# Half of layer 1 of four more blocks as seven multiplications, in the two PSUM banks of the plain groups

## The chip, the cores and the metric

The kernel runs on one core of a Trainium2 chip: TensorE (PE, matrix products, results only to PSUM), VectorE (DVE), ScalarE (ACT), GpSimd (POOL) and SyncE (SP, which here issues most DMAs). The metric is the device time of one execution in microseconds. A kernel's time is the median of its runs.

## The reference

Sliding-window causal attention (window 64, 8 batches, 8 heads, 576 tokens, head size 64), then a feed-forward layer with squared ReLU on the 4608 x 512 result.

```python
scores = (q @ k.T) / sqrt(64)                 # per batch and head
mask   = (rel >= 0) & (rel < 64)              # rel = row - column
attn   = softmax(where(mask, scores, -1e9))
x      = (attn @ v) as (4608, 512)            # tokens x (heads * 64)
h      = maximum(x @ w_in, 0.0)               # w_in:  512 x 2048
out    = (h * h) @ w_out                      # w_out: 2048 x 512
```

## The kernel before

**Blocks.** The tokens are handled in nine blocks of 512: block g below 8 is the first 512 tokens of batch g, block 8 gathers the last 64 tokens of every batch. Matmuls are in fp16 with fp32 sums. Inputs come in by DMA as fp32 into "st" tiles (ten buffers), POOL casts them to fp16 (L120), q and k are transposed by DMA (L242, issued by SP) into tiles of the pool tpool (tag "T", five buffers). The odd 64-token offsets of v need a second, shifted copy: six casts of 64 partitions on POOL for one block (shift_v_parts, L233).

**The main loop.** After a prologue for blocks 0 to 2, the loop over n = 1 to 8 does layer 2 of block n, layer 1 of block n+1 and attention of block n+2 in one step. The order on every engine is the order in which the code emits instructions. A string per step says which group is emitted at which slot: "1" a group of layer 1, "2" a group of layer 2. The dictionary "at", filled by put(i, work), holds what is emitted ahead of slot i: scores with their exp (Sc, L288 and L295), masking (M, L302), weighted sums and normalisation (A: L318, L325, L328), transposes of the result into xT (X, L344 and L118), and the sums that layers 1 and 2 need. Input parts are loaded a few at a time, by a running total over all slots (next_part).

**Layer 1, plain (F1).** A group f is 128 of the 2048 hidden features for 512 tokens: four matmuls of 512 columns into one of two PSUM banks (ps_f1, tag "f1"; L358), a ReLU on DVE into an "hr" tile (three buffers, L361), the square on ACT into h2 (L362). 16 groups make a block.

**Layer 1 in seven products (L1S).** In step 7 (layer 1 of block 8) x and w_in are cut into 2 x 2 pieces, and seven products of sums of pieces take the place of eight (the Winograd form). m is one of four sets of two groups of the first feature half and two of the second. Each product of a set (product1, L480) is four matmuls of 256 columns. The sums of pieces of w_in are W_sum, those of x are X_sum, both on DVE (L422). Products are added in PSUM in the order 5, 1, 6, 2, 7, 3, 4 over three banks a, b, c, with copies between banks by ACT (L118): product 5 is kept in SBUF (kept5), product 1 is copied from a to b, b to c after product 6, and c to a after product 7. done5 adds the kept product on DVE (L515). A list "later" puts off ReLUs and squares, and catch_up emits some after each group. In step 7 two sets go together, in the banks of attention and ps_f1.

**Layer 2 in seven products (L2S).** From step 2 on, layer 2 works likewise: for each of two token halves s, seven products of eight 256-column matmuls (L446), in the order 1, 2, 6, 5, 7, 3, 4, into the banks "chain" and "side". Its sums of h are S_sum (DVE, L422), 1024 columns each, four for each s; sums of w_out (T_sum) are made once in step 1. Scaled results go by ACT (L562) and DVE (L565) to the output tile.

**Where sums lie.** T sums fill the tile wsum, S sums of both halves fill hsum, W sums take four T tiles. S1 to S3 of s = 0 are made at the end of the step before.

## Time and profile before

| | |
|---|---|
| median of 3 runs | 296.46 us (296.03 to 297.95) |
| profiled execution | 298.29 us, its span 296.6 us |
| granted TensorE clock | 1.000 |
| busy: PE, DVE, ACT, POOL | 287.0, 225.5, 178.1, 126.7 us |
| layer 1, plain: L358 | 496 matmuls of 128x512, 122.7 us busy |
| layer 1, seven products: L480 | 112 matmuls of 128x256 |
| ReLU L361, square L362 | 0.686 and 0.630 us each |
| S sums L422 | 0.72 to 0.77 us each |

The span is the time from the first to the last instruction; the rest of an execution lies around it. Step 2 starts near 107 us, step 3 at 137, step 4 at 166, step 5 at 196, step 6 at 226, step 7 at 255 and step 8 at 280. Matmuls are pipelined, so a line of the timeline shows each longer than its share of PE; how long a run of them takes is read from one start to the next, or from the chain of work that ended last.

### The profile page before, as it was taken

The page shows a single profiled execution, that of the slowest core. Times are in us where ns is not written, and L with a number is a line of the kernel's source. Part 1 is how long each engine was busy: PE and PEld are TensorE (multiplying, and loading weights), DVE is VectorE, ACT ScalarE, POOL GpSimd, SP SyncE. Part 2 cuts the span into 40 slices and gives each one's busy share as a digit, 9 for nine tenths or more (in the row PEclk, how much of TensorE's full clock was granted, in tenths as well). Part 3 has the DMA queues.
Part 4 walks back from the last instruction along what each step waited for, and adds up shares of the span by engine and source line. Part 5 has one row for each costly group of instructions (what it writes and reads, how often), then busy time and mean ns, then how long its engine had stood idle before and what let it go on. Part 6 is the DMA issues. An engine that isn't in the chain of part 4 may idle for free.

```text
span 296.6 us, 7511 instructions
## 1 busy us (share of the span) xinstructions
PE 287.0 (97%) x2953; PEld 185.0 (62%) x2953; DVE 225.5 (76%) x395; ACT 178.1 (60%) x308; POOL 126.7 (43%) x215
## 2 busy tenths in 40 slices
PE   7889999999999999999999999999999999999994
PEld 5443445555545456666666666666666666888883
DVE  3667637679877788888778878887798889878781
ACT  3556667598465756575656465646564655687821
POOL 4567868973494358228416722923223000000002
PEclk9999999999999999999999999999999999999999
DMA  7899999999999997999899999899998014201015
GB/s 203 227 314 389 404 356 253 314 252 169 185 259 171 201 206 114 213 185 242 161 210 214 209 158 237 171 198 193 201 220 222 4 27 100 87 5 73 0 73 142
DMA packets 143651, 56.07 MB, mean 189 GB/s; under 512 B 127712, under 2 KB 136160, under 8 KB 143616
## 3 DMA queue, kind: packets, MB, share of 16 engines
q1 hardware_dynamic: 143232, 55.00, 86.0%
q0 software_dynamic: 144, 0.39, 0.6%
q8 instruction: 23, 0.38, 0.6%
q10 hardware_dynamic: 240, 0.20, 0.3%
q14 instruction: 12, 0.10, 0.1%
HBM read 38.80 MB, written 9.44 MB: 163 GB/s over the span
## 4 chain that ended last, share of the span: by engine, by line
PE 88%; SPq 6%; DMA 4%; POOL 1%; ACT 0%; issue 0%; DVE 0%
PE hps L358 34%; PE chain L446 14%; PE side L446 12%; PE ops L394 5%; PE at L480 4%; PE at L318 4%; DMA wsum<-in_moe_w_in_dram 4%; PE at L288 3%; PE side L394 2%; PE chain L394 2%; SPq L180 2%; PE more L446 2%; SPq L173 2%; PE at L344 2%; PE at L446 1%; PE tr L257 1%
## 5 line engine op out<-in xcount | busy, mean ns | idle before, releaser
L362 ACT ACTIVATE h<-hr 128x512 f16<-128x512 f32 x128 | 80.1, 630 | 80.0 <-DVE hr L361 79.6
L358 PE MATMUL hps<-xT,w_in_sb 128*128 128x512 f16 x496 | 122.7, 379 | 0.6 <-POOL w_in_sb L120 0.4
L361 DVE TENSOR_SCALAR hr<-hps 128x512 f32<-128x512 f32 x127 | 85.8, 686 | 31.3 <-PE hps L358 28.2
L358 PEld LDWEIGHTS <-w_in_sb 128*128 128x128 f16 x500 | 46.7, 98 | 43.2 <-issue 1.4
L446 PEld LDWEIGHTS <-hsum 128*128 128x128 f16 x448 | 43.0, 98 | 11.8
L120 POOL CAST v_ev<-st_v 128x512 f16<-128x512 f32 x31 | 22.3, 720 | 43.6 <-DMA st_v<-in_v_dram 43.6
L446 PEld LDWEIGHTS <-h 128*128 128x128 f16 x336 | 32.7, 98 | 8.3 <-issue 0.4
L120 POOL CAST k<-st_k 128x512 f16<-128x512 f32 x33 | 21.2, 644 | 36.6 <-DMA st_k<-in_k_dram 34.0
L295 ACT ACTIVATE pm<-at 128x1024 f16<-128x1024 f32 x35 | 34.1, 1015 | 2.2 <-PE at L288 2.2
L387 POOL DMA_DIRECT2D out_dram<-osb x3 | 1.8, 596 | 63.2 <-ACT osb L562 61.8
L328 DVE TENSOR_TENSOR xs<-at,rden 128x512 f16<-128x512 f32 x36 | 24.9, 691 | 1.2
L302 DVE TENSOR_TENSOR pm<-pm,mask 128x1024 f16<-128x1024 f16 x32 | 24.1, 765 | 2.0 <-ACT pm L295 1.9
L422 DVE TENSOR_TENSOR hsum<-h 128x1024 f16<-128x1024 f16 x28 | 21.6, 770 | 5.2 <-ACT h L362 5.1
L446 PE MATMUL chain<-wsum,hsum 128*128 128x256 f16 x192 | 24.9, 273 | 0.0
L233 POOL CAST v_od<-st_v 64x512 f16<-64x512 f32 x30 | 22.6, 755 | 1.6
L120 POOL CAST q<-st_q 128x512 f16<-128x512 f32 x28 | 19.2, 709 | 6.1 <-DMA qT<-q 3.5
L394 PEld LDWEIGHTS <-h 128*128 128x128 f16 x128 | 11.6, 98 | 12.2
L318 PEld LDWEIGHTS <-pm 128*64 128x64 f16 x576 | 11.2, 110 | 6.9 <-DVE pm L302 3.0
L118 ACT ACTIVATE xT<-at 128x512 f16<-128x512 f16 x22 | 12.8, 587 | 4.0 <-PE at L344 4.0
L394 PE MATMUL ops<-w_out_sb,h 128*128 128x512 f16 x64 | 14.8, 380 | 0.0
L318 PE MATMUL at<-v_ev,pm 128*64 128x65 f16 x384 | 13.7, 198 | 0.2 <-ACT v_ev L118 0.2
L562 ACT ACTIVATE osb<-chain 128x256 f32<-128x256 f32 x36 | 13.4, 372 | 0.3 <-PE chain L446 0.3
(118 smaller groups left out, 386.2 us busy)
## 6 DMA issues: line engine op xcount, KB each, us to landing
st_k<-in_k_dram SPq DMA_DIRECT2D x37, 256.0 KB, 3.9
out_dram<-osb SPq DMA_DIRECT2D x32, 256.0 KB, 3.1
st_q<-in_q_dram SPq DMA_DIRECT2D x29, 256.0 KB, 4.7
st_v<-in_v_dram SPq DMA_DIRECT2D x28, 256.0 KB, 4.1
w_st<-in_moe_w_in_dram SPq DMA_DIRECT2D x4, 512.0 KB, 6.2
wsum<-in_moe_w_in_dram SPq DMA_DIRECT2D x4, 512.0 KB, 10.2
hsum<-in_moe_w_out_dram SPq DMA_DIRECT2D x4, 512.0 KB, 7.9
wsum<-in_moe_w_out_dram SPq DMA_DIRECT2D x4, 512.0 KB, 9.2
```

Of the source, the lines that this page charges most:

```text
L120: engine.tensor_copy(out=out, in_=in_)
L233: nc.gpsimd.tensor_copy(out=od[g][to:to + 64, m, :, 0:D], in_=st["v", g, c][of:of + 64, :].rearrange("p (h d) -> p h d", h=H))
L295: nc.scalar.activation(out=p[:, hh, :] if apart else p[:], in_=sc[hh] if apart else both[:], func=AF.Exp, scale=1.0 / float(D) ** 0.5)
L302: nc.vector.tensor_tensor(out=p[:], in0=p[:], in1=m.unsqueeze(1).broadcast_to([P, 2, 512]), op=ALU.min)
L318: nc.tensor.matmul(a[jj * 64:(jj + 1) * 64, hh, jp * VW:jp * VW + D + 1], pm[g, hp][:, hh, j * 64:(j + 1) * 64], vsel, start=True, stop=True)
L328: nc.vector.tensor_tensor(out=x[:].rearrange("p j h d -> p h j d"), in0=a[:, :, :, 0:D], in1=rden[:].unsqueeze(3).broadcast_to([P, 2, 4, D ...
L358: nc.tensor.matmul(hps[:], w_in_sb[:, c, f * P:(f + 1) * P], xT[g][:, c, :], start=(c == 0), stop=(c == DMC - 1))
L361: nc.vector.tensor_scalar(out=hr[:], in0=hps[:], scalar1=0.0, scalar2=None, op0=ALU.max)
L362: nc.scalar.activation(out=h2[g][:, f, :], in_=hr[:], func=AF.Square)
L394: nc.tensor.matmul(f2[g, ts][:], h2[g][:, f, ts * P:(ts + 1) * P], w_out_sb[:, f, :], start=(f == 0), stop=(f == FFC - 1))
L422: (engine or nc.vector).tensor_tensor(out=out, in0=a, in1=b, op=op)
L446: nc.tensor.matmul(to, a[:, f, :], b[:, f, :], start=start and f == 0, stop=f == HF - 1, skip_group_check=True)
```

## The change

In steps 3 to 6 (layer 1 of blocks 4 to 7, the fifth to the eighth) the groups with f % 8 below 4 are made as two sets of seven products (pair_step), the other eight groups stay plain. In the order strings "7" is a product step. A set uses the two banks of ps_f1, with c in the place of a: product 7 is read by done5 before product 4 is added, and no copy from c to a is left. Product 5 is kept in columns 256 to 511 of w_out_sb, which only T_sum and the plain layer 2 of step 1 read; the results go to "hr" tiles. All ReLUs of done5 outputs are on ACT, at once after their group (two deferred ACT operations may follow each group).

S sums lie in half of hsum and are used for both s in turn, so those for s = 0 are now made at the start of their own step, those for s = 1 after the products of s = 0. The last block's s = 1 has the other half of hsum, in which W sums of the first two sets lie before. W sums of the other two sets lie in two T tiles. X sums lie in the "qk" tiles.

In the steps with product steps attention starts at slots 2 and 20 of 36, with longer distances to masking, weighted sums and transposes. The shifts of v come behind the third q cast of the next block.

```diff
-    S_sb = hsum[:].bitcast(FP16).rearrange("p a b -> p (a b)").rearrange("p (k c d) -> p k c d", k=4, c=8)
+    S_sb = hsum[:, 0:4, :].bitcast(FP16).rearrange("p a b -> p (a b)").rearrange("p (k c d) -> p k c d", k=4, c=8)
+    S2_sb = hsum[:, 4:8, :].bitcast(FP16).rearrange("p a b -> p (a b)").rearrange("p (k c d) -> p k c d", k=4, c=8)
...
-    def s_of(k, s):
-        return S_sb[:, k - 1, :, 128 * s:128 * s + 128]
+    def s_of(k, two=False):
+        return S2_sb[:, k - 1] if two else S_sb[:, k - 1]
...
@@ -432,14 +433,15 @@
             minus(t_of(4), b_of(1, 0), t_of(2))
 
     def S_sum(g, k, s):
+        w = g == B and s == 1
         if k == 1:
...
+    def W_sum(k, pair):
+        if (pair, k) not in wsums:
+            if pair == 0:
+                t = hsum[:, 3 + k, :].bitcast(FP16)
+                wsums[pair, k] = t.rearrange("p (c f) -> p c f", c=2)
+            else:
+                t = tpool.tile([P, HP, 512], FP16, name="wS", tag="T")
+                for i in range(2):
+                    wsums[pair, k + i] = t[:, 2 * i:2 * i + 2, :]
+        cols = slice(pair * 512, pair * 512 + 512)
+        w = wsums[pair, k]
+        a, b, op = {1: (w_of(1, 0)[:, :, cols], w_of(1, 1)[:, :, cols], ALU.add),
+                    2: (wsums.get((pair, 1)), w_of(0, 0)[:, :, cols], ALU.subtract),
+                    3: (w_of(0, 0)[:, :, cols], w_of(1, 0)[:, :, cols], ALU.subtract),
+                    4: (w_of(0, 1)[:, :, cols], wsums.get((pair, 2)), ALU.subtract)}[k]
+        minus(w, a, b, op)
 
     def X_sum(g, k):
...
         if k not in xsums:
-            t = apool.tile([P, 2, 512], FP16, name="xS", tag="pm", bufs=4)
-            xsums[k] = t[:, 0, :].rearrange("p (c t) -> p c t", c=2)
+            t = apool.tile([P, 2, 512], FP16, name="xS", tag="qk")
+            for i in range(2):
+                xsums[k + i] = t[:, i, :].rearrange("p (c t) -> p c t", c=2)
         a, b = {1: (x_of(g, 0, 1), x_of(g, 0, 0)), 2: (x_of(g, 1, 1), xsums.get(1)),
                 3: (x_of(g, 1, 1), x_of(g, 0, 1)), 4: (x_of(g, 1, 0), xsums.get(2))}[k]
         minus(xsums[k], a, b)
...
+                w = wsums[m // 2, a][:, cc, f % 512:f % 512 + P] if isinstance(a, int) else a[:, cc, f:f + P]
+                nc.tensor.matmul(to[:, u * HX:(u + 1) * HX], w, b[:, cc, :],
...
-    kept5 = {}
...
-        def piece32(name):
-            return stp.tile([P, 512], FP32, name=name, tag="st")
+        def piece32():
+            return opool.tile([P, 512], FP32, name="hr", tag="hr")
+
+        def five(m):
+            t = w_out_sb[:, 4 * (m % 2):4 * (m % 2) + 4, HC:2 * HC].bitcast(FP32)
+            return t
...
         def done(m, i, j, bank):
-            hr = piece32("ls")
+            hr = piece32()
...
         def done5(m, i, j, bank, relu_on_act):
-            y = piece32("ls")
-            nc.vector.scalar_tensor_tensor(out=y[:], in0=bank, scalar=1.0, in1=kept5[m][:],
+            y = piece32()
+            nc.vector.scalar_tensor_tensor(out=y[:].rearrange("p (a b) -> p a b", a=4),
+                                           in0=bank.rearrange("p (a b) -> p a b", a=4), scalar=1.0, in1=five(m),
                                            op0=ALU.mult, op1=ALU.add)
             if relu_on_act:
                 later["act"].append(lambda: nc.scalar.activation(out=y[:], in_=y[:], func=AF.Relu))
...
-        to, lhs, rhs, start = {5: (1, wsums.get(1), xsums.get(1), True), 1: (0, w_of(0, 0), x_of(g, 0, 0), True),
-                               2: (0, w_of(0, 1), x_of(g, 1, 0), False), 6: (1, wsums.get(2), xsums.get(2), False),
-                               7: (2, wsums.get(3), xsums.get(3), False), 3: (1, wsums.get(4), x_of(g, 1, 1), False),
-                               4: (0, w_of(1, 1), xsums.get(4), False)}[p]
+        to, lhs, rhs, start = {5: (1, 1, xsums.get(1), True), 1: (0, w_of(0, 0), x_of(g, 0, 0), True),
+                               2: (0, w_of(0, 1), x_of(g, 1, 0), False), 6: (1, 2, xsums.get(2), False),
+                               7: (2, 3, xsums.get(3), False), 3: (1, 4, x_of(g, 1, 1), False),
+                               4: (2, w_of(1, 1), xsums.get(4), False)}[p]
         for m in two:
             product1(banks[m % 2][to], m, lhs, rhs, start)
         for m in two:
             a, b, c = banks[m % 2]
             if p == 5:
-                kept5[m] = piece32("p5")
-                copy(nc.scalar, kept5[m][:], b)
+                copy(nc.scalar, five(m), b.rearrange("p (a b) -> p a b", a=4))
...
             elif p == 6:
                 copy(nc.scalar, c, b)
             elif p == 7:
-                copy(nc.scalar, a, c)
-                later["dve"].append(lambda m=m, c=c: done5(m, 1, 1, c, m < 2 or RELU[0]))
+                done5(m, 1, 1, c, RELU[0])
             elif p == 3:
-                later["dve"].append(lambda m=m, b=b: done5(m, 0, 1, b, RELU[1]))
+                done5(m, 0, 1, b, RELU[1])
             else:
-                done(m, 1, 0, a)
-
-    RELU = (True, False)
+                done(m, 1, 0, c)
+
+    RELU = (True, True)
+    open_pair = {}
+
+    def pair_step(g, p, m):
+        if p == 5:
+            b, a = [ps_f1.tile([P, 512], FP32, name="hps", tag="f1") for _ in range(2)]
+            open_pair[m] = a[:], b[:], a[:]
+        L1S(g, p, (m,), {m: open_pair[m]})
...
+        pending, unshifted = [], []
...
                 elif g < B and c == 3:
-                    shift_v_parts(g)
+                    unshifted.append(g)
+                if unshifted and w == "q" and c == 2 or unshifted == [g3]:
+                    shift_v_parts(unshifted.pop())
                 behind = len(load_list) - len(parts_left) - 1
...
         def A(g, hp, i=1):
+            if g in unshifted:
+                shift_v_parts(unshifted.pop())
             AV(g, hp, i)
             N(g, hp)
 
...
         done = 12
+        HYB = (3, 4, 5, 6)
+        BURST = (2, 20)
+        WPUTS = {2: ((3, 1, 0), (12, 2, 0), (17, 3, 0)), 6: ((10, 1, 1), (20, 2, 1), (24, 3, 1), (30, 4, 1)), 3: ((0, 4, 0),)}
+        MAT, AT, XAT = ((4, 6), (8, 8), (10, 12))
+        SPUTS = ((2, 1, 0), (4, 2, 0), (6, 3, 0), (7, 4, 0), (18, 1, 1), (18, 2, 1), (23, 4, 1), (25, 3, 1))
+        XPUTS = ((1, 2), (2, 3), (12, 4))
...
+            apart, both = n == NBLK - 2, n in HYB
+            steps = []
             if apart:
                 cs = [ps_f1.tile([P, 512], FP32, name="c", tag="f1") for _ in range(2)]
                 three = [(at_ps[0][:, i, :], at_ps[1][:, i, :], cs[i][:]) for i in range(2)]
-                first = [lambda p=p, two=two: L1S(one, p, two, three)
+                steps = [lambda p=p, two=two: L1S(one, p, two, three)
                          for two in ((0, 1), (2, 3)) for p in (5, 1, 6, 2, 7, 3, 4)]
-            else:
-                first = [] if last else [lambda f=f: F1(one, f) for f in range(FFC)]
-            order = ("22222222" + 8 * "112" if n == 1 else
+            elif both:
+                steps = [lambda p=p, m=m: pair_step(one, p, m) for m in range(2) for p in (5, 1, 2, 6, 7, 3, 4)]
+            first = ([] if last or apart else
+                     [lambda f=f: F1(one, f) for f in range(FFC) if not both or f % HF >= 4])
+            order = ("22222222112112112112112112112112" if n == 1 else
                      "2" * 14 if last else
-                     "11221121122122" * 2 if apart else
-                     ("2112121212121211" if n == 2 else "1212121212121211") + "21212121121122")
-            a, b = iter(first), iter(second)
-            fill = [next(a if c == "1" else b) for c in order]
+                     "77227727722722" * 2 if apart else
+                     "111127272772277272" * 2 if both else
+                     "211212121212121121212112111222")
+            kinds = {"1": iter(first), "2": iter(second), "7": iter(steps)}
+            fill = [next(kinds[c]) for c in order]
             at = {}
...
             if n == 1:
                 put(0, lambda: Sc(g2, 3), lambda: A(g2, 2))
-                put(2, lambda: M(g2, 3))
+                put(3, lambda: M(g2, 3))
                 put(3, lambda: X(g2, 2, own=1))
                 put(5, lambda: A(g2, 3))
                 put(7, lambda: X(g2, 3, own=1))
-                for i, k in ((1, 1), (3, 2), (6, 3), (8, 4)):
+                for i, k in ((0, 1), (3, 2), (5, 3), (8, 4)):
                     put(i, lambda k=k: T_sum(k))
             else:
                 for i, k, s in (((0, 1, 0), (0, 2, 0), (3, 3, 0), (4, 1, 1), (5, 2, 1), (6, 4, 0), (9, 3, 1), (10, 4, 1)) if last else
-                                ((2, 4, 0), (4, 1, 1), (6, 2, 1), (12, 3, 1), (19, 4, 1)) if apart else
-                                ((2, 4, 0), (4, 1, 1), (6, 2, 1), (9, 3, 1), (18, 4, 1))):
+                                ((0, 1, 0), (0, 2, 0), (1, 4, 0), (4, 3, 0), (10, 1, 1), (13, 2, 1), (17, 3, 1), (23, 4, 1)) if apart else
+                                SPUTS if both else
+                                ((0, 1, 0), (3, 2, 0), (3, 3, 0), (4, 4, 0), (13, 1, 1), (18, 2, 1), (21, 3, 1), (21, 4, 1))):
                     put(i, lambda k=k, s=s: S_sum(g, k, s))
-            if not last:
-                end = len(fill) - 1
-                if not apart:
-                    put(24 if n == 1 else 20, lambda: S_sum(one, 3, 0))
-                if not apart:
-                    put(end if n == 1 else end - 1, lambda: S_sum(one, 1, 0))
-                    put(end, lambda: S_sum(one, 2, 0))
+            end = len(fill) - 1
             base = 4 * (n + 2)
-            for i, two in zip((11, 22) if n == 1 else (9, 20) if n == 2 else (9, 17) if n == 6 else (8, 19),
+            for i, two in zip((11, 22) if n == 1 else (8, 20) if n == 2 else BURST,
                               (units[base:base + 2], units[base + 2:base + 4])):
                 for t, u in enumerate(two):
                     if u is not None:
                         put(i, lambda u=u, t=t: Sc(*u, i=t))
-                        put(i + 3 + t, lambda u=u: M(*u))
-                        put(i + 6, lambda u=u, t=t: A(*u, i=t))
-                        put(i + (7 if u[0] == B else 8 + t), lambda u=u, t=t: X(*u, own=t))
-            for i, k, cc in {NBLK - 4: ((19, 1, 0), (22, 1, 1)),
-                             NBLK - 3: ((2, 2, 0), (9, 2, 1), (17, 3, 0), (26, 3, 1)),
-                             NBLK - 2: ((3, 4, 0), (17, 4, 1))}.get(n, ()):
-                put(i, lambda k=k, cc=cc: W_sum(k, dve, cc))
-            if n == NBLK - 3:
-                put(25, lambda: X_sum(seq[-1], 1))
-            if apart:
-                for i, k in ((0, 2), (2, 3), (4, 4)):
+                        put(i + ((3, 4) if n == 1 else (2, 4) if n == 2 else MAT)[t], lambda u=u: M(*u))
+                        put(i + ((6, 6) if n == 1 else (6, 6) if n == 2 else AT)[t], lambda u=u, t=t: A(*u, i=t))
+                        put(i + ((8, 9) if n == 1 else (8, 9) if n == 2 else XAT)[t], lambda u=u, t=t: X(*u, own=t))
+            for i, k, pair_ in WPUTS.get(n, ()):
+                put(i, lambda k=k, pair_=pair_: W_sum(k, pair_))
+            if n + 1 in HYB or n + 1 == NBLK - 2:
+                put(end + 1 - 2, lambda: X_sum(seq[n + 2], 1))
+            if hybrid:
+                for i, k in ((2, 3), (3, 2), (8, 4)) if apart else XPUTS:
                     put(i, lambda k=k: X_sum(one, k))
             for i, group in enumerate(fill):
-                if last and i == 0:
+                if i == 0:
                     catch_up()
                 for work in at.pop(i, []):
                     work()
-                total = 12 + (30 * (n - 1) + i + 1) * (len(load_list) - 12) // 140
+                total = 12 + (36 * (n - 1) + i + 1) * (len(load_list) - 12) // 168
                 while done < total and (parts_left or pending):
                     next_part()
                     done += 1
                 group()
-                catch_up(1, 1)
-            assert not at, at.keys()
+                catch_up(1, 2)
+            for i in sorted(at):
+                for work in at[i]:
+                    work()
```

31 lines of the change are left out of this document (11 added, 20 removed).

## The prediction

> **What bounds the kernel now.** I read the page first, then the waits of TensorE (PE), the chain that ended last, the busy time by stretch and the timeline of one stage. "Step n" is one pass of the main loop: layer 2 of block n, layer 1 of block n+1, attention of block n+2, blocks counted from 0. The seven-product form now reaches layer 1 of blocks 4 to 7 (5 to 8 counted from 1), so steps 3, 4, 5 and 6, and half of the 16 feature groups there; step 7 had it before.
>
> From the page, then all waits of PE's matmuls, then the chain, then two stretches (busy us and count of PE, PEld, DVE, ACT, POOL; clock, DMA share, GB/s):
>
> ```profile
> PE 287.0 (97%) x2953; PEld 185.0 (62%) x2953; DVE 225.5 (76%) x395; ACT 178.1 (60%) x308; POOL 126.7 (43%) x215
> ...
> PE busy L100 <- POOL ident masks.py:199: 1.4, 1, 1.4
> PE tr L257 <- DVE q L120: 0.8, 2, 0.6
> PE hps L374 <- ACT xT L118: 0.5, 1, 0.5
> ...
> 189.33 1.73 PE hps L358 x8
> ...
> 257.18 0.87 PE chain L446 x8
> 258.06 0.87 PE side L446 x8
> 258.93 1.75 PE at L480 x16
> ...
> 166.00:196.00 30.00, 30.00 (x325) 20.22 (x323) 23.88 (x42) 17.70 (x33) 15.41 (x24) 1.00 1.03 183
> 226.00:255.00 29.00, 29.00 (x306) 19.05 (x304) 25.67 (x47) 16.42 (x30) 0.62 (x1) 1.00 0.23 63
> ```
>
> PE's waits sum to 5 us and all lie in the first 60 us. From there to the last matmul at 292 us the matmuls follow one another, at the full granted clock. A step is as long as its matmuls: about 29.5 us in steps 2 to 6. Eight 512-column matmuls take 1.73 (0.216 each), sixteen 256-column ones of the seven-product form 1.75 (0.109 each). DVE is busy 24 to 26 us of a step, ACT 16 to 18: time taken off PE is gained only if these two still deliver on time.
>
> **The gain.** In each of the four steps eight plain groups go (32 matmuls x 0.216 = 6.91 us) and 14 product steps come (2 pairs of groups x 7 products, 4 matmuls of 256 columns each: 56 x 0.1094 = 6.13). That is 0.79 us a step, **3.15 us** in all, and the most the change can give, since PE has no other idle time between 60 and 292 us. Layer 2 keeps its 112 matmuls a step, attention its scores, its weighted sums and its transposes, each in two bursts.
>
> **Work added beside PE.** Per half step (one pair): three ACT copies (products 5, 1, 6; 0.59 each by the L118 rows of step 7) and two ACT ReLUs (0.625). The four rectifications and four squares replace those of four plain groups one for one. DVE gets two X sums per half (0.42 each). The eight W sums (0.68 each) existed before, in steps 5 to 7; three now lie in step 2, one in step 3, four in step 6. Instructions that are ready behind another start sooner than their full time: by the trace's starts a square occupies ACT for 0.54 (0.63 full), an exp for 0.90 (1.015), a layer-2 scaling for 0.26 (0.37), and DVE a rectification for 0.60 (0.686). Per half of about 14.3 us of PE work that makes ACT 10.7 and DVE 11.6; in step 6, with its four W sums, DVE about 12.9. No engine exceeds PE in the sum. So the question is order, not load.
>
> **The walk through one half.** Time 0 is its first matmul; PE without waits: plain groups end at 0.86 and 1.73; scores of two heads pairs (0.57); plain groups end at 3.16 and 4.03; layer-2 product 1 at 4.90; product 5 at 5.34; layer-2 product 2 at 6.21; product 1 at 6.65; layer-2 product 6 at 7.52. Then product 2 adds into bank a, which ACT must first have copied to bank b.
>
> When is that copy done? A reader starts 0.24 after the matmuls nominally end (PE 202.50, DVE 202.74 in step 5). The second group's rectification starts at 2.04, behind an X sum, and ends at 2.73; its square starts at 2.77; the two exps are queued behind it, at 3.31 and 4.21; then two squares from 5.12, the scaling at 6.19, product 5's copy at 6.46, product 1's copy. Whether the last two overlap decides the margin. In step 7 of before:
>
> ```profile
> 256.39 1.08 ACT L118 ACTIVATE p<-at 128x512 f32<-128x512 f32 x2 [0.54 <-PE at L480]
> ...
> 257.51 1.20 ACT L118 ACTIVATE at<-at 128x512 f32<-128x512 f32 x2
> ```
>
> The first "at<-at" writes the bank that a copy before it reads, and starts at 257.51, after both copies are over (256.39 + 1.08 = 257.47). So here the copy runs from 7.09 to 7.68 and product 2 starts at about 7.76: **0.24 us lost**. In the second half there is no X sum ahead and I take 0.17. Bounds: with overlap 0.08; with no overlap anywhere in that queue (all full durations) the copy ends at 8.24, 0.80 lost. I take the value by the step-7 rows, since they are this very pair. Eight halves: 4 x 0.24 + 4 x 0.17 = 1.64 us.
>
> The Trainium skill, "ScalarE: Activation LUTs", section "What ACT_TABLE_LOAD costs", says that back-to-back ACTIVATEs overlap by about 93 ns. Squares here do (0.63 against 0.54); the two copies above do not. By the rule alone the loss would be 0.08 x 8 = 0.6 and the time near 294.9.
>
> The second tight place is the masking of the second head pair (L302), on DVE now behind four hidden-sum operations instead of spread ones. In steps 3 to 5 POOL casts inputs and shifts v at that time, and the sums are slower: in the stretch 107.1 to 196 the "hsum<-h" form has a median of 0.889 against 0.680 in step 6. From the fourth rectification (over at 4.88): S2 0.64, S3 0.80, mask 0.70, addition 0.33, S4 0.60, mask 0.78 give 8.73; PE, already 0.24 late, wants it at 8.5. **0.25 lost** in the first halves of steps 3 to 5, 0.75 together (bounds: 0 with quiet sums, 0.9 each if every sum takes the 1.14 that is the longest row). The second halves have one sum less there and step 6 a quiet POOL: nothing.
>
> **Moved edits, and what hides them.** S sums of a block's first half now come at the start of its own step. S1 and S2 are needed by layer-2 product 6 at 6.65 and are done by 5.6; uncovered, each microsecond late would be one on PE. In step 7, S1 must wait for the last square of step 6 (about 1.1 into the step), then come S2, S4 and two X sums (X3, X2), done at 3.7, while product 6 wants X2 at 3.5: 0.2 lost. In step 7 four PSUM copies (0.585) leave ACT, and four ReLUs and squares come in place of four DVE squares (0.68): ACT rises to some 22 of 25 us of full durations, with the last bank reuse still about 0.2 ahead; I count nothing. Step 2 gets four S sums and three W sums; S2 is done at about 4.1 when product 6 wants it at 4.34: nothing, up to 0.4 if POOL slows it.
>
> Scores move forward to slot 2 of the step, so the transposed k must be there some 5 us earlier. In step 2 the last transpose of the next block's k is issued by 132.3 and needed at 138.7: covered. The shifts of v (six POOL casts, 4 to 6 us) fall behind three q casts, 2 us later: for step 3 about 141 against first use at 145; POOL's own followers are the next q's fourth cast and its k. That move helps the SP queue, where a q transpose (L242) sits behind those shifts and everything after it waits:
>
> ```profile
> 110.28 1.12 SPq L209 DMA_DIRECT2D st_k<-in_k_dram  x1
> 115.17 1.20 SPq L242 DMA_TRANSPOSE qT<-q  x1
> ...
> SPq L242 <- POOL q L120: 19.1, 7, 4.8
> ```
>
> Up to 19 us of SP's waiting can go, but PE waits for no input now, so it is worth nothing by itself. No DMA is added. The ten input tiles (st) keep v 2 us longer, and layer 1 of step 7 no longer borrows from them. Product 5 now lies in columns of w_out that nothing reads after step 1.
>
> **The sum.** Span 296.57 - 3.15 + 1.64 + 0.75 + 0.2 = 296.0, that is 0.55 less. The profiled execution took 298.29 in all, 1.7 outside its span and 0.6% above the median of the runs (296.46); I carry the difference over: **295.9 us**. About 1%, or 3 us, is what a measurement of this kernel can tell from no change.
>
> **Rivals.** (1) *The banks are served in time.* ACT overlaps, the masks are early, and the full 3.15 stays: 293.3, 1.06% faster. For it: load of ACT under 75% and no wait of PE in step 7 of before. Against: the queue walked above has no slack, while step 7 has two pairs per product and twice the time. Chance of over 1% faster 0.13.
>
> (2) *ACT's queue takes PE's place* in each half: product 1's copy stands behind a square, two exps, two squares, a scaling and a copy. With full durations each half loses 0.84 (copy 8.24, release 8.32, hand-over 0.04): 296.46 - 3.15 + 8 x 0.84 + 0.2 = 300.2. It cancels the gain from 0.37 a half and is over 1% slower from 0.74. For it: relu and square of one tile cannot overlap each other, and every wait of a group pushes the next. Against: 0.54 between squares, in 76 places. Chance 0.10.
>
> (3) *DVE and POOL block each other.* The mask and S sums of the first halves each wait for a cast: five of them at 1.14 in place of about 0.70 add 2.2, of which the slack leaves about 1.9 in steps 3 to 5: 295.9 + 3 x 1.7 = 301. For it: rows of 1.14 exist; against: medians of 0.68 for masks. Chance 0.07. The Trainium skill, "SBUF — State Buffer", section "SBUF: two separate sides", says of the port pair that DVE and GpSimd share that the loser blocks for the other's whole instruction; the spread 0.68 to 1.14 agrees, and by that rule alone every sum that meets a cast would pay.
>
> (4) *The moved input is late*: a shift or k transpose after its use stops PE outright; margins of 4 to 6 us speak against it; it belongs to the slower cases, inside their 0.17.
>
> **How the numbers follow.** Within 1%: 0.70, my forecast and its neighbours; faster 0.13 (rival 1, its ceiling hardly beyond the bound); slower 0.17 (rivals 2 to 4). Range 293.3 (rival 1) to 299.2 (two thirds of the way from forecast to rivals 2 and 3): about a tenth is left out on each side.
>
> **What would show it.** After: L358 with 32 matmuls a step less in steps 3 to 6, L480 with 56 more; PE waits of 0.1 to 0.3 at product 2 on ACT's copy (L118) in every half, and at the weighted sums (L318) on DVE's mask; SP's wait of L242 on POOL down from 19 us; steps 3 to 6 at 29.2 to 29.5 us. Wrong if PE shows no wait there (then 293.3), or waits over 0.7 a half, or any wait on a DMA or a v shift.

## The result, and the profile after

The changed kernel takes **300.45 us** (median of 15 runs, 298.12 to 301.5), the one before 296.99 (15 runs on the same chip): a ratio of 1.010, 95% interval 1.0078 to 1.0122. It is about 1% slower, and 1.25 us above the top of my range. The median span went from 295.35 to 298.0, and what lies outside the span from 1.70 to 2.43.

The profile of before that the prediction read (span 296.57) was one of the longer executions of that kernel, so I compare stretches. A step is taken from the end of its predecessor's last layer-2 product to that of its own (steps 1 and 2 together from the first layer-2 matmul). In us, from the two profiled executions:

| | steps 1+2 | 3 | 4 | 5 | 6 | 7 |
|---|---|---|---|---|---|---|
| before | 62.04 | 29.76 | 29.76 | 29.80 | 29.05 | 24.70 |
| after | 62.72 | 31.33 | 29.90 | 30.21 | 28.23 | 25.29 |
| difference | +0.68 | +1.57 | +0.14 | +0.41 | -0.82 | +0.59 |

The differences add up to +2.57. The head before step 1 varies by about 2 us between executions (2.2 between the two profiled ones of the kernel before); the tail behind step 7 is 16.6 in both. One more caution: steps 3 to 5 differ between executions of the same code. They sum to 89.32 here for before and to 90.02 in its second profile (e0); the order of the change gave 91.44 here and 90.74 and 90.53 in two variants that leave these steps alone (e2, e8). Differences under 1 us in these sums say nothing by themselves.

Step 6 gained what the products promise; every other step lost (steps 4 and 5 by no more than executions differ). The page's line of busy times now reads:

```profile
PE 285.4 (96%) x3049; PEld 194.5 (65%) x3049; DVE 231.8 (78%) x407; ACT 201.8 (68%) x352; POOL 125.1 (42%) x215
```

In the view of all waits (us in total, times, longest; line numbers are one higher than before up to the product code) these lines answer to those of before:

```profile
PE at L319 <- DVE pm L303: 2.5, 3, 1.3
PE at L345 <- DVE xs L329: 0.4, 1, 0.4
PE chain L448 <- ACT w_out_sb L119: 0.2, 1, 0.2
...
SPq L243 <- POOL q L121: 10.5, 7, 2.4
```

PE's 96 additional matmuls are 224 of 256 columns more and 128 of 512 columns fewer. Its busy time fell, and the span did not. A wait that did not exist before stands on top: weighted sums (L319) wait for a mask (L303), 2.5 us in three waits. Counted from matmul to matmul, with the small ones, they are 1.5, 0.46 and 1.01 in the first halves of steps 3, 4 and 5 and 0.19 each in the second halves of steps 3 and 4: 3.3 us. SP's wait on POOL fell from 19.1 to 10.5 as foreseen; no step shows a gain from it.

Stretches by engine (busy us and count of PE, PEld, DVE, ACT, POOL; clock, DMA share, GB/s): the two stretches that the prediction shows of before, now in after, then the first half of step 3 and the first half of step 6:

```profile
166.00:196.00 30.00, 29.63 (x347) 22.55 (x346) 26.27 (x47) 22.97 (x42) 13.77 (x23) 1.00 1.17 196
226.00:255.00 29.00, 29.00 (x338) 22.28 (x336) 27.18 (x52) 21.76 (x40) 0.00 (x0) 1.00 0.19 54
...
136.80:153.27 16.47, 15.06 (x174) 11.23 (x172) 14.93 (x26) 10.30 (x20) 10.89 (x15) 1.00 1.33 185
228.24:242.36 14.12, 14.12 (x167) 10.79 (x165) 13.07 (x27) 10.57 (x20) 0.00 (x0) 1.00 0.22 59
```

The same half of the form takes 14.12 us without POOL and 16.47 with it. DVE has one instruction less in the slow one and is busy 1.86 longer; the clock is 1.00 in both. Here is that first half of step 3 in the timeline (start, us, engine, line, operation; what PE waited for in brackets):

```profile
137.80 4.61 POOL L234 CAST v_od<-st_v 64x512 f16<-64x512 f32 x6
...
142.40 0.68 DVE L423 TENSOR_TENSOR hsum<-hsum,h 128x1024 f16<-128x1024 f16 x1
142.47 1.08 POOL L121 CAST q<-st_q 128x512 f16<-128x512 f32 x1
...
143.00 1.09 DVE L423 TENSOR_TENSOR hsum<-h 128x1024 f16<-128x1024 f16 x1
...
143.50 4.11 POOL L121 CAST k<-st_k 128x512 f16<-128x512 f32 x4
...
144.02 1.09 DVE L303 TENSOR_TENSOR pm<-pm,mask 128x1024 f16<-128x1024 f16 x1
...
145.03 0.41 DVE L587 SCALAR_TENSOR_TENSOR osb<-side,osb 128x256 f32<-128x256 f32 x1
145.37 0.76 DVE L423 TENSOR_TENSOR hsum<-h,hsum 128x1024 f16<-128x1024 f16 x1
...
146.05 1.09 DVE L303 TENSOR_TENSOR pm<-pm,mask 128x1024 f16<-128x1024 f16 x1
...
147.20 0.25 PE L319 MATMUL at<-v_ev,pm 128*64 128x65 f16 x4 [1.33 <-DVE pm L303]
```

And the same place in step 6:

```profile
233.85 0.68 DVE L423 TENSOR_TENSOR hsum<-h 128x1024 f16<-128x1024 f16 x1
...
234.45 0.69 DVE L303 TENSOR_TENSOR pm<-pm,mask 128x1024 f16<-128x1024 f16 x1
...
235.39 0.68 DVE L423 TENSOR_TENSOR hsum<-h,hsum 128x1024 f16<-128x1024 f16 x1
...
235.99 0.69 DVE L303 TENSOR_TENSOR pm<-pm,mask 128x1024 f16<-128x1024 f16 x1
```

Beside casts, sums and masks take up to 1.09 in place of 0.68. Where the chain that ended last was PE alone before, it now runs through DVE, in step 5 for instance (start, us, what):

```profile
203.26 1.20 DVE hsum L423 x2
204.46 1.01 DVE pm L303
205.47 0.33 DVE osb L587
205.81 0.52 DVE hsum L423
206.33 1.11 DVE pm L303
...
207.48 0.44 PE at L319 x16
```

### The profile page after: what moved, and what is told of

Same layout as the page of the kernel before. It is cut to its first block, busy times and chain, and to the rows that moved or that the text cites. A ratio compares the mean times of both kernels' runs of the same rounds, so it can differ in the third digit from the quotient of the medians.

```text
span 298.3 us, 7774 instructions
## 1 busy us (share of the span) xinstructions
PE 285.4 (96%) x3049; PEld 194.5 (65%) x3049; DVE 231.8 (78%) x407; ACT 201.8 (68%) x352; POOL 125.1 (42%) x215
## 4 chain that ended last, share of the span: by engine, by line
PE 37%; DMA 24%; SPq 15%; POOL 9%; ACT 8%; DVE 3%; issue 3%; POOLq 0%; DVEq 0%
PE hps L359 8%; DMA st_k<-in_k_dram 7%; DMA st_q<-in_q_dram 6%; DMA st_v<-in_v_dram 6%; SPq L243 6%; PE ops L395 5%; PE side L448 4%; PE chain L448 4%; POOL v_od L234 4%; DMA wsum<-in_moe_w_in_dram 4%; SPq L210 3%; PE hps L492 3%; ACT h L521 3%; PE more L448 2%; POOL k L121 2%
## 5 line engine op out<-in xcount | busy, mean ns | idle before, releaser
L359 PE MATMUL hps<-xT,w_in_sb 128*128 128x512 f16 x368 | 88.4, 379 | 0.8 <-POOL w_in_sb L121 0.6
L363 ACT ACTIVATE h<-hr 128x512 f16<-128x512 f32 x96 | 59.2, 630 | 35.2 <-DVE hr L362 34.8
L362 DVE TENSOR_SCALAR hr<-hps 128x512 f32<-128x512 f32 x95 | 64.4, 688 | 23.7 <-PE hps L359 20.1
L359 PEld LDWEIGHTS <-w_in_sb 128*128 128x128 f16 x372 | 34.7, 98 | 37.4 <-POOL w_in_sb L121 1.9
L448 PEld LDWEIGHTS <-hsum 128*128 128x128 f16 x448 | 43.4, 98 | 6.4
L121 POOL CAST v_ev<-st_v 128x512 f16<-128x512 f32 x31 | 20.7, 668 | 45.8 <-DMA st_v<-in_v_dram 45.8
L521 ACT ACTIVATE h<-hr 128x512 f16<-128x512 f32 x48 | 28.9, 626 | 12.5 <-DVE hr L525 11.7
L121 POOL CAST k<-st_k 128x512 f16<-128x512 f32 x33 | 24.0, 736 | 22.3 <-DMA st_k<-in_k_dram 18.5
L303 DVE TENSOR_TENSOR pm<-pm,mask 128x1024 f16<-128x1024 f16 x32 | 25.8, 807 | 2.0 <-ACT pm L296 1.9
L534 ACT ACTIVATE hr<-hr 128x512 f32<-128x512 f32 x24 | 14.9, 622 | 11.8 <-DVE hr L530 11.8
L234 POOL CAST v_od<-st_v 64x512 f16<-64x512 f32 x30 | 20.1, 668 | 1.6
L319 PEld LDWEIGHTS <-pm 128*64 128x64 f16 x576 | 11.6, 110 | 9.1 <-issue 4.2
L319 PE MATMUL at<-v_ev,pm 128*64 128x65 f16 x384 | 14.8, 198 | 2.7 <-DVE pm L303 2.5
L492 PEld LDWEIGHTS <-hsum 128*128 128x128 f16 x160 | 14.7, 98 | 2.0
```

The lines of the kernel that those rows point to most:

```text
L121: engine.tensor_copy(out=out, in_=in_)
L234: nc.gpsimd.tensor_copy(out=od[g][to:to + 64, m, :, 0:D], in_=st["v", g, c][of:of + 64, :].rearrange("p (h d) -> p h d", h=H))
L303: nc.vector.tensor_tensor(out=p[:], in0=p[:], in1=m.unsqueeze(1).broadcast_to([P, 2, 512]), op=ALU.min)
L319: nc.tensor.matmul(a[jj * 64:(jj + 1) * 64, hh, jp * VW:jp * VW + D + 1], pm[g, hp][:, hh, j * 64:(j + 1) * 64], vsel, start=True, stop=True)
L359: nc.tensor.matmul(hps[:], w_in_sb[:, c, f * P:(f + 1) * P], xT[g][:, c, :], start=(c == 0), stop=(c == DMC - 1))
L362: nc.vector.tensor_scalar(out=hr[:], in0=hps[:], scalar1=0.0, scalar2=None, op0=ALU.max)
```

## The experiments

My theory: POOL's casts stretch DVE's instructions with two inputs in SBUF, and the change puts too many of these ahead of the masks; less of either brings steps 3 to 5 back to some 29 us (29.76 less the gain of 0.79). The rival: the sequence is short of time anyway, and a repair only moves the wait. In the table, "stretch" is what the two-input fp16 instructions of steps 3, 4, 5, 6 took beyond 0.680 (1024 elements) or 0.418 (512) each, summed from the trace. Ratios are against the kernel before, with 95% intervals; for e4 there is a single time.

| version | us | ratio | steps 3, 4, 5, 6, 7 | stretch in 3, 4, 5, 6 |
|---|---|---|---|---|
| before | 296.99 | 1 | 29.76, 29.76, 29.80, 29.05, 24.70 | 0.9, 0.9, 1.0, 0.3 |
| after | 300.45 | 1.010 [1.0078, 1.0122] | 31.33, 29.90, 30.21, 28.23, 25.29 | 3.3, 1.3, 1.6, 0.1 |
| e1_masks | 299.37 | 1.0079 [1.0051, 1.0107] | 30.63, 30.13, 29.60, 28.97, 25.57 | 2.6, 1.3, 0.7, 0.1 |
| e2_kept5 | 299.66 | 1.0078 [1.0051, 1.0106] | 30.53, 30.04, 30.17, 28.23, 25.27 | 2.0, 2.1, 1.5, 0.1 |
| e4_pool6 | 303.0 | | 30.90, 30.66, 29.14, 30.38, 25.28 | 2.8, 2.7, 0.8, 2.2 |
| e5_shift | 299.5 | 1.0083 [1.005, 1.0116] | 30.64, 30.22, 29.97, 28.24, 25.28 | 2.5, 2.4, 1.1, 0.1 |
| e7_noshift | 298.13 | 1.0018 [0.9991, 1.0044] | 29.70, 30.40, 29.92, 28.23, 25.28 | 1.0, 2.4, 1.3, 0.0 |
| e8_step7 | 303.93 | 1.0214 [1.0182, 1.0245] | 30.89, 29.79, 29.85, 28.23, 28.69 | 2.8, 1.5, 1.1, 0.1 |
| e3b_noprod | 300.59 | 1.0104 [1.0076, 1.0131] | 30.22, 31.27, 30.25, 29.94, 24.95 | 0.8, 2.1, 1.0, 0.1 |
| e12_relief | 298.61 | 1.0027 [1.0006, 1.0048] | 29.34, 29.35, 29.26, 29.13, 26.50 | 2.3, 2.2, 1.2, 0.0 |
| e13_best | 295.76 | 0.9951 [0.9932, 0.9971] | 29.65, 29.50, 29.01, 28.22, 25.28 | 2.6, 1.8, 0.9, 0.0 |
| e14_seam | 294.96 | 0.9935 [0.9912, 0.9957] | 29.21, 29.13, 29.37, 28.23, 25.36 | 2.8, 2.3, 1.4, 0.0 |
| e15_relu | 299.32 | 1.0078 [1.0052, 1.0105] | 30.86, 30.27, 30.03, 28.23, 25.28 | 3.1, 2.6, 1.2, 0.0 |

**e0_before**: the kernel before, unchanged, profiled again.

> The kernel before, unchanged, against itself, to learn its spans. The profile of before has a span of 296.57 us and 1.7 us outside it, that of after 298.33 and 2.45; their medians differ by 3.46, the spans by 1.76 only. Theory A (the profiled execution of before was a slow one, and each execution of after has 0.7 us more outside its span): spans of this kernel have a median near 295.3, 1.7 below the median time. Rival B (nothing outside the span differs): the time exceeds the span by 2.4 here too, and the spans lie near 294.6.

297.06, ratio 0.9994 [0.9973, 1.0014]; its spans have a median of 295.35, with 1.72 outside. So the 296.57 that my sum started from was 1.2 above the median span, and the 1.70 outside belongs to that kernel, not to the execution. Its steps 3 and 5 took 30.20 and 30.06 (29.76 and 29.80 above), step 5 with a wait of 0.2 on a mask.

**e4_pool6**: POOL's casts brought into the quiet step 6, the order kept. The added casts go to a tile that nothing reads.

```diff
+load_list += [(g, "z", c) for g in (4, 5, 6, 7) for c in range(4)]   # z: v again, cast by POOL
```

> The changed kernel with 16 more loads of v parts, each cast by POOL into a tile that nobody reads, four at the end of step 5 and twelve in step 6, where POOL is idle otherwise. It tells whether POOL makes the masks late. Theory A (DVE's fp16 operations with two SBUF inputs take up to 1.09 us in place of 0.68 beside a POOL cast): in step 6 such long operations appear and its weighted sums wait for the mask; step 6 grows from 28.2 to 28.7 or more. Rival B (order and load alone): step 6 stays at 28.2 to 28.3, and its operations at 0.68.

Step 6 rose from 28.23 to 30.38, with 2.18 of stretch where there had been 0.06. PE's waits in that stretch (228.4 to 258.8; total, times, longest) show the same line as step 3 of after; there it stands at L322:

```profile
POOL spare L121 <- DMA st_z<-in_v_dram: 16.2, 12, 7.3
...
PE at L322 <- DVE pm L306: 1.9, 2, 1.1
```

This is the cause on its own: same instructions, same order on DVE, PE and ACT, only casts, and the loads that feed them, beside them. The loads are no rival: in steps 3 to 5 of after, where loads run too, the 12 sums and masks that meet no cast take 0.691 at most.

**e1_masks**: the masks moved ahead of the S sums.

```diff
-SPUTS = ((2,1,0), (4,2,0), (6,3,0), (7,4,0), (18,1,1), (18,2,1), (23,4,1), (25,3,1))
+SPUTS = ((2,1,0), (4,2,0), (9,3,0), (11,4,0), (18,1,1), (18,2,1), (27,4,1), (27,3,1))
```

> The changed kernel with both masks of a burst ahead of the S3 and S4 sums: S3 from slot 6 to 9 and S4 from 7 to 11 in the first half, both to slot 27 in the second. Theory A (masks of the second pair come late, behind sums that POOL makes slower): the waits of the weighted sums on the mask in steps 3, 4 and 5 (1.5, 0.46 and 1.01 us, with 0.19 twice beside them) go, steps 3 to 5 fall to about 29.3 us, the time falls by 2.5 to 3, to about 297.7 (from 300.45). Rival B (the two engines are just too full in a half, whatever the order): the lateness moves to the rectification and the bank copy behind the sums, product 6 or 7 waits in place of the weighted sums, and the time falls by less than 1.

The mask wait is gone, and another wait of equal size stands one link further, where the transposition of the attention output waits for its scaling by DVE:

```profile
PE at L345 <- DVE xs L329: 2.5, 4, 0.8
```

Steps 3 to 5 fell by only 1.08 together, to 90.36, which is 0.2 below e8, where their order is that of the change: a gain is not shown. Step 6 gave back 0.74, since its layer-2 product 3 now waited for S4 and the layer-1 product behind it for a rectification. Here the rival was right: order alone moves the lateness.

**e15_relu**: the rectification of product 2 on ACT, the order as in the change.

```diff
-nc.vector.tensor_scalar(out=hr[:], in0=bank, scalar1=0.0, scalar2=None, op0=ALU.max)
+if len(two) == 1 and p == 2 and g < 7:
+    nc.scalar.activation(out=hr[:], in_=bank, func=AF.Relu)
+else:
+    nc.vector.tensor_scalar(out=hr[:], in0=bank, scalar1=0.0, scalar2=None, op0=ALU.max)
```

> The changed kernel with one edit: the ReLU of product 2 in steps 3 to 5 on ACT in place of DVE. It stands behind the second mask in DVE's queue and ahead of the normalisations. Theory A (the order of masks and sums and the load behind them are two places of one overload, and both must go): the waits on the mask stay (about 3 us in steps 3 to 5) since nothing ahead of the mask changes, steps 3 to 5 stay within 0.6 of 91. Rival B (total load of DVE alone): steps 3 to 5 fall by 2 or more by this edit alone.

Steps 3 to 5 sum to 91.16, within the 90.53 to 91.44 of the change's own order, and the mask wait is what it was:

```profile
PE at L319 <- DVE pm L303: 2.6, 3, 1.3
```

Less load behind the masks does nothing for the masks. Step 2, which this edit leaves alone, once waited 0.6 for a shift of v here, the only such wait that I saw: the margins of 4 to 6 us that I had given the moved inputs can be used up.

**e12_relief**: both together (e1's order, e15's rectification, here in step 6 too), with later W sums in steps 2 and 6 and, at the start of step 7, product 5 kept in a tile of its own and one rectification on DVE.

```diff
+if len(two) == 1 and p == 2: nc.scalar.activation(out=hr[:], in_=bank, func=AF.Relu)
-WPUTS = {2: ((3,1,0), (12,2,0), (17,3,0)), 6: ((10,1,1), (20,2,1), (24,3,1), (30,4,1)), ...
+WPUTS = {2: ((3,1,0), (18,2,0), (24,3,0)), 6: ((14,1,1), (19,2,1), (31,3,1), (34,4,1)), ...
```

> The changed kernel with masks ahead of S3 and S4, and four more edits in places of their own: the ReLU of product 2 on ACT in place of DVE (0.6 us less on DVE, 0.5 more on ACT in each half); W sums of step 2 later (slots 18 and 24); W sums of step 6 later; the seam to step 7 as in the kernel with product steps in step 6 alone. Theory A (in steps 3 to 5 DVE, lengthened by POOL, is the bound): steps 3 to 5 fall by 1.5 to 2.5 together against the kernel with the masks ahead (90.4), step 2 loses its 0.55 wait, step 7 falls to 24.8; the time to about 297, that of before. Rival B (ACT is as short as DVE in a half): the copy of product 1 or of product 6 comes late in place of the masks, and steps 3 to 5 stay over 89.8.

Steps 3 to 5 are 87.95, against 91.44 in after and 90.36 in e1, although the casts still stretch DVE by 2.3, 2.2 and 1.2. Only 0.24, 0.23 and 0.23 at product 2 remain there. Much of it was given back behind them. W3 and W4 at slots 31 and 34 of step 6 stand ahead of the X sum that step 7 begins with, whose wait follows; and step 6, where order, rectification and W sums were all changed, lost what it had gained. Which of the three did that was not separated.

```profile
PE at L492 <- DVE xS L423: 1.1, 1, 1.1
```

**e13_best**: the repair of e12 in steps 3 to 5 only; steps 6 and 7 as in the change.

```diff
+SPUTS3 = ((2,1,0), (4,2,0), (9,3,0), (11,4,0), (18,1,1), (18,2,1), (27,4,1), (27,3,1))   # n = 3 to 5
+if len(two) == 1 and p == 2 and g < 7: nc.scalar.activation(out=hr[:], in_=bank, func=AF.Relu)
-WPUTS = {2: ((3,1,0), (12,2,0), (17,3,0)), ...
+WPUTS = {2: ((6,1,0), (18,2,0), (24,3,0)), ...
```

> The changed kernel with, in steps 3 to 5 only, the masks ahead of S3 and S4 and the ReLU of product 2 on ACT; W sums of step 2 at slots 6, 18 and 24 (from 3, 12 and 17); steps 6 and 7 exactly as changed. Theory A (DVE's queue was the loss in steps 3 to 5, and the two late edits at the seam cost steps 6 and 7 of the run before 2.1 us): steps 3 to 5 at 29.3 each, step 6 at 28.2, step 7 at 25.3, steps 1 and 2 together 0.3 over before's 62.0; the span 1 to 1.4 under before, the time 0.3 to 1.2 under it. Rival B (step 6 and 7 are short only because the steps before them were long): they grow by more than 0.5, and the time is that of before.

295.76, ratio 0.9951: faster than the kernel before by about half a per cent, and than the change by 4.7 us. Steps 1 and 2 fell to 62.14, steps 3 to 5 to 88.16. The same half of step 3 in its timeline:

```profile
141.46 0.67 DVE L423 TENSOR_TENSOR hsum<-hsum,h 128x1024 f16<-128x1024 f16 x1
142.06 1.09 DVE L303 TENSOR_TENSOR pm<-pm,mask 128x1024 f16<-128x1024 f16 x1
...
143.41 0.76 DVE L303 TENSOR_TENSOR pm<-pm,mask 128x1024 f16<-128x1024 f16 x1
144.09 1.09 DVE L423 TENSOR_TENSOR hsum<-h 128x1024 f16<-128x1024 f16 x1
```

The durations are as long as in after, 1.09 where POOL holds them up, but the second mask ends at 144.17, where it ended at 147.14 (this half began 0.94 earlier). The stretch remains; it has slack to fall into. Both edits together are far outside what executions differ by: steps 3 to 5 take 87.95, 88.16 and 87.71 in e12, e13 and e14.

**e5_shift** and **e7_noshift**: the shifts of v back at once behind their casts; and none for blocks 5 to 7, whose weighted sums then read unshifted data (this part of the result differs).

```diff
-unshifted.append(g)
+shift_v_parts(g)                     # e5
-elif g < B and c == 3:
+elif g < 5 and c == 3:               # e7, with AV reading v_ev there
```

> The changed kernel with the shifts of v right behind the casts of v again, as before. In the trace of after the six shift casts of step 3 run from 137.8 to 142.4, beside the X sums, S1 and the casts of the next block, in the half that loses 1.5 us at the second mask. Theory A (where POOL's burst lies decides): the shifts lie some 2 us earlier, partly in the step before, step 3 falls by 0.7 or more, the time by 0.5 to 1.5, although SP waits for POOL again. Rival B (the amount of POOL work in the half decides, not its place): steps 3 to 5 stay within 0.4 of 91.4 together.

> The changed kernel without the shifts of v of blocks 5 to 7 (the weighted sums of these blocks read the unshifted copy in their place, so their output differs): POOL has six casts, some 4.5 us, less in each of steps 3 to 5; the same matmuls, the same DVE and ACT operations in the same order. Theory A (POOL makes DVE late in the first halves): the waits of the weighted sums on the mask fall from 3.3 us to under 1.2, steps 3 to 5 from 91.4 to 89.3 or less, the time by about 2. Rival B (order and load of DVE alone): steps 3 to 5 stay over 90.7.

In e5 step 3 fell by 0.69, step 4 rose by 0.32 and step 5 fell by 0.24, with 2.5, 2.4 and 1.1 of stretch. This looks like stretch that moves with the casts, but e2, which leaves steps 3 to 5 alone, differs from after in the same way (30.53, 30.04, 30.17, with 2.0, 2.1 and 1.5): e5 shows no effect of the shifts' place. In e7 step 3, with 1.0 of stretch left, took 29.70, below the 30.53 to 31.33 of after, e2 and e8, while step 4 at 2.4 took 30.40; mask waits of 0.68, 1.19 and 0.90 stayed in steps 3 to 5 beside the casts of q and k. Without these shifts the median is 298.13, 2.3 below the change and still over e13: they are part of the load, not all of it.

**e2_kept5** and **e8_step7**: step 7. e2 keeps product 5 of that step in a tile that nothing else uses; e8 starts step 7 with a layer-2 product.

```diff
+kept5[m] = stp.tile([P, 512], FP32, name="p5", tag="st")      # e2
-"77227727722722" * 2 if apart else
+"27722772772722" * 2 if apart else                            # e8
```

> The changed kernel with product 5 of step 7 kept in input tiles again, as before, in place of columns of w_out; steps 3 to 6 stay. Theory A: the first layer-2 product of each half of step 7 waits for ACT's copies into w_out (0.26 and 0.38 us at its second matmul), though it reads other columns of the same rows: these waits go, step 7 falls from 25.29 to 24.7, the time by about 0.6. Rival B: product 1 would wait for ACT anyway, at the next bank copy, and step 7 stays over 25.1.

> The changed kernel with another order of step 7: its first layer-2 product ahead of the first product steps, and its third ahead of product 6 (per half L P5 P1 L L P6 P2 L P7 P3 L P4 L L in place of P5 P1 L L P6 P2 L P7 P3 L L P4 L L). At the start of step 7 ACT still has a ReLU and three squares of step 6, until 257.8 in the profile, so that the copies of products 5 and 1 end at 260.3 and PE waits before. Theory A (ACT's backlog at the seam): with 0.87 us more ahead of product 5 and of product 6 the two waits (0.26 and 0.38) go, step 7 falls from 25.3 to 24.8 or less, the time by 0.5. Rival B (ACT is short throughout step 7): product 4 or product 6 waits in another place and step 7 stays over 25.1.

In after, the first layer-2 product of step 7 stops at its second matmul until ACT has written the columns of w_out_sb that hold product 5, columns that this matmul doesn't read:

```profile
257.95 1.07 ACT L119 ACTIVATE w_out_sb<-at 128x512 f32<-128x512 f32 x2
258.22 1.34 PE L448 MATMUL chain<-w_out_sb,h 128*128 128x256 f16 x8
```

e2 removed those two waits (0.26 and 0.38), and product 6 waited 0.33 and 0.46 for ACT's copies instead: step 7 stayed at 25.27. e8 (303.93) failed for a reason of its own: its product lands behind product 4 on the chain's bank and waits for ACT to scale that:

```profile
PE chain L448 <- ACT osb L584: 3.6, 2, 2.2
```

**e14_seam**: e13 with e2's tile, one rectification and square of product 3 back on DVE, and step 7's first X sum earlier.

```diff
+kept5[m] = stp.tile([P, 512], FP32, name="p5", tag="st")
-done5(m, 0, 1, b, RELU[1])
+done5(m, 0, 1, b, RELU[1] and not (len(two) == 1 and m == 1 and g == 7))
-put(end + 1 - 2, lambda: X_sum(seq[n + 2], 1))
+put(30 if n == 6 else end + 1 - 2, lambda: X_sum(seq[n + 2], 1))
```

> The same, and at the seam to step 7 product 5 in input tiles, the last ReLU and square of product 3 on DVE as one operation, and the first X sum of step 7 four slots earlier (30). Theory A (step 7 is long because ACT still works off step 6; taking 1.2 us off its queue there lets the first copies keep up, if the X sum is not pushed back): step 7 from 25.3 to 24.8, step 6 within 0.2 of 28.3. Rival B (DVE in step 6 has no room either): step 6 or the first product of step 7 loses what is won.

294.96; its interval overlaps e13's, so the two are not told apart. Step 7 is 25.36, and the second half, far from the seam, waits as long as the first (0.42, 0.46). What queues ahead of these copies on ACT was not tried further.

```profile
PE at L492 <- ACT at L119: 0.5, 2, 0.3
```

**e3_noprod**, **e3b_noprod**, **e9_only6**: no products in layer 1 of blocks 4 to 7, with step 2's order and then with the one of before; and products in step 6 only.

```diff
-HYB = (3, 4, 5, 6)
+HYB = ()       # e3: step 2's order in steps 3 to 6; e3b: "1212121212121212..." as before; e9: (6,)
```

> The change without its product steps in steps 3 to 6: plain groups there again, in the order and with the attention slots of step 2 (bursts at 8 and 20); S sums in one buffer, W sums, moved shifts and the new step 7 stay. Theory A (the loss comes from the product halves): steps 3 to 6 at 29.8, 29.8, 29.8 and 29.1 as before, step 7 back near 24.7 because no ReLUs and squares of product steps stand in ACT's queue at its start, step 2 still 0.5 above before, the time within 0.7 of before; and the time outside the span, 1.7 before and 2.4 after, is 1.7 if it belongs to the instructions of the product steps. Rival B (S sums in one buffer, made at the start of their own step, cost as much): steps 3 to 6 at 30.3 or more and the time 2 over before.

> As the kernel without product steps, but with steps 3 to 6 in the order of before, which begins with a plain group: the earlier order put the first layer-2 product of a step right behind the last one of the step before, on the same bank, and lost 0.64 us in each of four steps to the scaling on ACT. S sums stay in one buffer at the start of their own step, the shifts and step 7 stay changed. Theory A (the loss comes from the product halves): steps 3 to 6 at 29.8, 29.8, 29.8, 29.1 within 0.2, step 2 still 0.5 long, step 7 at 24.9, the time within 0.9 of before, 1.7 us outside the span. Rival B (the S sums, now all beside POOL's casts at the start of a step, or the moved shifts cost by themselves): steps 3 to 5 over 30.2.

> Product steps only in step 6, where POOL casts nothing; steps 3 to 5 plain in the order of before; W sums of the first two sets in steps 3 to 5, none in step 2; in step 7 product 5 in input tiles, and the last ReLU and square before the seam on DVE in one operation. Theory A: step 6 at 28.2 to 28.4 without waits (29.05 before), steps 3 to 5 at 29.8, step 2 at 29.8, step 7 at 24.7 because ACT's queue is 1.1 us shorter at the seam: the span 0.8 under before, 0 to 0.3 more outside it, the time 0.5 to 0.8 under before. Rival B (step 6 only passes its lateness on): step 7 or step 6 gains back what the other loses, and the time is that of before or higher.

e3 (300.26, 1.0091 [1.0063, 1.0118]) was spoilt by my order: each step lost 0.64 at its start, on the same bank as in e8. e3b shows that the rest of the change costs without the products: with S sums of a block's first half at the start of their own step, beside POOL, steps 3 to 5 take 30.22, 31.27 and 30.25, up to 1.5 above before, with waits on masks and on copies into xT. Step 6, where POOL is idle, took 29.94, 0.89 above before, with waits on rectifications. At 300.59 this kernel is no faster than the change: so much can be lost without a single product step. e9 (303.5, 1.0194 [1.0168, 1.022]) is worse still (32.10 and 31.59 in steps 4 and 5, which also make W sums there; what those sums add was not separated), and its late W sums push step 7's X sum as in e12.

## Why the prediction was wrong

- **The failed step is the price of the masks**: "0.25 lost in the first halves of steps 3 to 5, 0.75 together". They cost 1.5, 0.46 and 1.01 there, and 0.19 in two second halves, for which I had "nothing": 3.3 in all (about 3.4 in e2 and 2.9 in e8). Most of the place and the reason (casts beside sums) were right, and the term was mis-sized by 2.6, more than half of the miss. I walked that queue with durations of 0.60 to 0.80, near the medians of before, where such work was spread over the step. In after POOL works almost without a gap from 137.80 to 147.61, and what stands ahead of the second mask was X2 0.87, X3 0.82, S3 1.09, the first mask 1.09, S4 0.76 and the mask itself 1.09. Even my upper bound, 0.9 a half, is below the 1.5, and it was summed wrongly: with its three S sums at 1.14, as it says, the 8.73 of the walk becomes 10.11, which is 1.6 behind the 8.5, not 0.9. The waits of 1.5 and 1.01 are the "over 0.7 a half" that I had named as a sign of being wrong. Rival 3 named this mechanism with 0.07, at 301, 0.55 above what came.
- **The gain of 3.15** is right where it can be seen: 0.82 in step 6, against 0.79 predicted. Against that, steps 3 to 5 of e12 are on average still 0.35 above 28.97 (29.76 less 0.79), two thirds of it the wait at product 2.
- **The wait at product 2** came in four halves of eight, 0.24, 0.16, 0.23 and 0.21: 0.84 in place of 1.64. That each is near my 0.24 is luck, since I let ACT's queue alone make it, in every half. The lines below are the second X sum, the second group's rectification, the copy of product 1 and product 2, in the first halves of step 3 and of step 6.

```profile
138.47 0.87 DVE L423 TENSOR_TENSOR xS<-xT,xS 128x512 f16<-128x512 f16 x1
139.26 0.68 DVE L362 TENSOR_SCALAR hr<-hps 128x512 f32<-128x512 f32 x1
...
144.26 0.58 ACT L119 ACTIVATE hps<-hps 128x512 f32<-128x512 f32 x1
...
144.89 0.60 PE L492 MATMUL hps<-xT,w_in_sb 128*128 128x256 f16 x4
...
229.91 0.41 DVE L423 TENSOR_TENSOR xS<-xT,xS 128x512 f16<-128x512 f16 x1
...
230.25 0.69 DVE L362 TENSOR_SCALAR hr<-hps 128x512 f32<-128x512 f32 x1
...
235.25 0.58 ACT L119 ACTIVATE hps<-hps 128x512 f32<-128x512 f32 x1
...
235.89 0.60 PE L492 MATMUL hps<-xT,w_in_sb 128*128 128x256 f16 x4
```

In step 6 the copy does not overlap the one before it, as I had walked, and ends 7.59 after the half's first matmul; product 2 starts at 7.65, and PE loses nothing. So it is in all four halves without the wait. In the other four a sum that a cast stretched (0.87 for 0.41 here) makes that rectification end 0.14 to 0.45 later, and the exps behind its square, and the copy, are late by the same amount; PE waits for it, less what it has lost on the way. This loss too is DVE beside POOL.

- **Step 7** lost 0.59, not 0.2. I walked to the X sums and missed that, in this program, a copy into w_out_sb holds up a matmul that reads other columns of the same rows. e2 shows that ACT's copies are the next limit there anyway.
- **Step 2** lost 0.68 where I had nothing, "up to 0.4 if POOL slows it": 0.55 of it is the wait of the attention transposes (L345) on DVE, behind W2 at slot 12 (1.09 beside a cast) and S1. I had walked to S2 only. With W2 at slot 18 in e13 steps 1 and 2 lose 0.10.
- **Outside the span** I carried 1.70 over; it was 2.43. Every run of the change has more than any run of before (2.15 at least against 1.81 at most). Without products in steps 3 to 6 it is 1.76 (e3) and 1.69 (e3b), in e13 2.06 and in e14 1.79. What makes it is open.
- **Covered as predicted**: no wait of PE on a load or, in the change's profile, on a shift of v; the shorter wait of SP shows no gain.

With the measured terms the sum is -3.15 + 0.84 + 3.3 + 0.59 + 0.68 = +2.3, against +2.57 by steps and +2.65 by median spans; the 0.7 outside brings these to 3.3 and 3.4, near the measured 3.46.

## What to carry to other kernels

Sum the load of an engine over a step and you see whether it fits; to see whether it is on time, walk each queue to the consumer with the duration that each instruction has while its neighbours work there, not with a mean over another schedule. When added work makes a wait, put the urgent instruction ahead and also take load off what follows it: each repair alone (e1, e15) left most of the loss in steps 3 to 5, both together removed most of it. Keep a repair to the stages that need it: the later W sums of step 6 in e12 cost step 7 over a microsecond. And profile the same code twice before reading a difference of less than a microsecond from two profiles.

## What the hardware showed

DVE's two-input SBUF instructions and POOL's casts take turns. In after 24 of the sums and masks of 1024 elements in steps 3 to 6 overlap a POOL cast and take 0.865 on average, up to 1.122; the 28 that don't take 0.683, at most 0.691. It is not every meeting that costs DVE: 12 of the 24 keep 0.675 to 0.694, and the 12 longer ones all began while a cast was running and end 0.54 after it. So not every sum that meets a cast pays, as I had put it under rival 3. The casts pay too (0.61 alone, up to 1.15 beside a sum). Instructions that read a PSUM bank are not held up: the additions to the output tile take 0.41 to 0.43 beside a cast (9 of them, that of 145.03 among them) and without one (15). The Trainium skill, "SBUF — State Buffer", section "SBUF: two separate sides", describes the port pair that DVE and GpSimd share as a lock held for a whole instruction. The timeline agrees: the q cast at 142.47 outlasts the sum of 142.40 and ends at 143.55, and the next sum, begun at 143.00, ends 0.54 later.

How little the stretch itself says was not expected either: with 2.3, 2.2 and 1.2 of it e12's steps 3 to 5 take 29.3 each, and with 1.3 step 4 of after takes 29.90. In these runs it costs only what it pushes past the next use.
